# RWKV attention and GELU MLP on one core: a drain of TensorE between state and value products, replaced by a GpSimd memset that both sides wait on

## The chip, the cores and the metric

The kernel runs on one core of a Trainium2 chip. The metric is the device time of one execution in microseconds; where runs are compared, it is the median of several. The core has five engines with instruction queues of their own: TensorE (PE, matrix products; its weight loads are shown apart as PEld), VectorE (DVE), ScalarE (ACT), GpSimd (POOL) and SyncE (SP, which issues the loads and stores here). They wait for each other by semaphores only.

## What is computed

A recurrent attention over 768 tokens, for 4 batches of 8 heads of 48 channels, and an MLP with a GELU behind it, all in float32:

```python
for t in range(S):
    kt, vt, rt = (k[:, :, t], v[:, :, t], r[:, :, t])
    cur = np.einsum('bhd,bhe->bhde', u[None] * kt, vt)
    y[:, :, t] = np.einsum('bhd,bhde->bhe', rt, state + cur)
    state = w[None, :, :, None] * state + np.einsum('bhd,bhe->bhde', kt, vt)
# x: y with the heads of a token side by side, 3072 x 384
h = x @ w_in                       # 384 x 2048
g = 0.5 * h * (1.0 + erf(h / np.sqrt(2.0)))
return g @ w_out                   # 2048 x 384
```

## The kernel before

The recurrence is worked out in chunks. A **group** is one pair of heads over one chunk of 128 tokens, for all four batches; there are 6 chunks x 4 pairs = 24 groups. Within a group everything is matrix products of 48 or 64 rows on 64x64 corners of the array, in two halves of 64 tokens:

- `scores` (line 403): keys times receptances, 16 products into the PSUM banks `A` (and `own`, 16 more of the same shape, in the groups of the first two chunks). `select` then copies the entries of the past into `Am`.
- `old` (line 422): the **state products**, the state so far (`Sa`, `Sb`) times the receptances (`Tb`), 16 products of 48 rows into the bank pair `Y`.
- `new` (line 432): the **value products**, `Am` times the values (`Nb`), 16 products of 64 rows that add into the same places of `Y`. The two kinds use different rows of the array and write the same banks of `Y`; a drain stands ahead of them (line 433), which holds TensorE's queue until all products before it have ended.
- `gains` (line 415): keys times values, what the chunk adds to the state.

float32 products are two passes, so 16 products are 32 entries of the trace.

TensorE works on the MLP nearly all the time (products of 128x128 with 512 columns, lines 554 and 596: the high and low halves of activations and weights, three times each). Between them it makes a **visit** to the recurrence: `products(g, f)` (line 506) is one block of TensorE's work for two neighbouring groups, the state and value products of the earlier one, `g`, and the scores and gains of the next, `f`. The order in the block is state products of `g`, scores of `f`, drain, value products of `g`, gains of `f`. The first visit has no `g`, the last no `f`; the 19 between have both. The first four groups are worked in a prologue (`first_group`) with a block `old, new` each, without scores between.

The order on each engine is fixed when the kernel is built: `Plan` takes every block with its estimated time and what it reads and writes, plays the machine through, and writes the instructions of each queue in the order of that play. GpSimd's part in the main loop is three products of 128x384 for each group (lines 379, 381, 391), which wait for the group's load `Nb` and are needed by the visit where that group is `f` or later. The two buffers of `Nb` and `Tb` alternate: the load of the group after `f` goes into those of `g`, and waits in SP's queue until the visit has read them.

Of the kernel before, what the change touches and what calls it, by code (L numbers as in the profile page):

```python
# [9 lines left out]
F32 = mybir.dt.float32  # L10
# [17 lines left out]
HALF = 64  # L28
# [17 lines left out]
class Plan:  # L46
# [9 lines left out]
    def add(self, eng, ns, at, fn, r=(), w=()):  # L56
        n = len(self.ops)
        deps = set()
        for x in r:
            deps.add(self.writer.get(x))  # L60
            self.readers.setdefault(x, []).append(n)
        for x in w:
            deps.add(self.writer.get(x))
            deps.update(self.readers.pop(x, ()))
            self.writer[x] = n
        deps -= {None, n}
        self.ops.append((eng, ns, at, fn, deps))
        self.reads.append(set(r))
# [65 lines left out]
def rwkv_gelu_mlp(tc, rkT, rkv, wuT, uN, wmlp, r, k, vT, w, u, out):  # L134
    nc = tc.nc
    with ExitStack() as ctx:
        cst = ctx.enter_context(tc.tile_pool(name="cst", bufs=1))
# [6 lines left out]
        def sb(shape, dt, name, pool=None):  # L144
            return (pool or wk).tile(shape, dt, name=name)
# [130 lines left out]
        one = lambda x, i: x[:, :, i:i + 1]  # L276
# [73 lines left out]
        quarter = lambda x: slice(64 * x, 64 * x + D)  # L350
        heads = lambda x: slice(D * x, D * x + D)
        times = lambda h: slice(64 * h, 64 * h + 64)
# [50 lines left out]
        def scores(g, keys=None, col=0):  # L403
            for b in range(NB):
                for h in range(2):
                    for x in range(2):
                        k_ = (g.t[:, 1] if keys is None else keys)[quarter(x), b, times(h)]
                        nc.tensor.matmul(g.x[times(h), x, col + b * HALF:col + (b + 1) * HALF], lhsT=k_,  # L408
                                         rhs=g.t[quarter(x), 0, b, times(h)], start=True, stop=True)

        def own(g):
            scores(g, g.kb, U0)


        def gains(g):
            for b in range(NB):
                for x in range(2):
                    for h in range(2 if g.more else 1):
                        nc.tensor.matmul(g.u[quarter(x), h, g.u0 + b * D:g.u0 + (b + 1) * D], lhsT=g.kn[times(h), b, heads(x)],  # L419
                                         rhs=g.vn[times(h), b, heads(x)], start=True, stop=True)  # L420

        def old(g):
            for b in range(NB):
                for j in range(2):
                    for h in range(1 if g.c == 0 else 0, 2):
                        l = quarter(j ^ h)
                        nc.tensor.matmul(g.y[quarter(j), h, b * HALF:(b + 1) * HALF], lhsT=g.s[h][l, b, :],  # L427
                                         rhs=g.t[l, 0, b, times(h)], start=(b == 0 and not spreads(g)), stop=False,
                                         skip_group_check=True)


        def new(g):
            nc.tensor.drain()
            for b in range(NB):
                for j in range(2):
                    for h in range(2):
                        nc.tensor.matmul(g.y[quarter(j), h, b * HALF:(b + 1) * HALF], lhsT=g.vn[times(h), b, heads(j ^ h)],  # L437
                                         rhs=g.am[times(h), j ^ h, b, :], stop=True, skip_group_check=True,
                                         start=(g.c == 0 and h == 0 and b == 0 and not spreads(g)))


        spreads = lambda g: g.c == 0 and g.p < 3
# [63 lines left out]
        def products(g, f):  # L506


            r, w, ns = [], [], 0
            if g:  # L510
                r += [g.T, g.V, g.AM] + g.S[0] + g.S[1]
                w += g.Y
                ns += 1200
            if f:
                r += [f.T, f.K, f.V] + ([f"{f.KB}0", f"{f.KB}1"] if f.direct else [])
                w += f.X + f.U
                ns += 1300 if f.direct else 850

            def go():
                if g:  # L520
                    old(g)
                if f:
                    scores(f)
                    if f.direct:
                        own(f)
                if g:
                    new(g)
                if f:
                    gains(f)

            add("pe", ns, LATER, go, r=r, w=w)
# [57 lines left out]
        bank = lambda i: O[i] if i < 3 else YU[:, 0]  # L589
# [175 lines left out]
        with tc.If(plain[0] < 2 * LP * NP):  # L765
# [5 lines left out]
            g = general.enter_context(tc.tile_pool(name="g", bufs=2))  # L771
# [76 lines left out]
```

## Time and profile before

| | |
|---|---|
| time, median of 3 runs | 507.44 us (504.56 to 509.48) |
| span of the profiled execution | 507.7 us |
| TensorE busy with products | 486.0 us, 96% of the span |
| VectorE, ScalarE, GpSimd busy | 243.0, 205.5, 71.6 us |
| value products of the 19 visits with a next group, first start | 52.2, 73.1, 94.3, 113.7, 136.1 ... 406.5 us |
| one visit on TensorE | 2.2 us (405.25 to 407.46 in the one at 406 us) |

A row of the timeline gives a start, a length, an engine, a line of the kernel, what is written from what, and in brackets the idle time ahead of it with what ended it. Weight loads run ahead of the products that they belong to, so they overlap the products before. "Issue" stands for time in which the engine waited for nothing that the profile shows; a drain shows up as that. The ends of matrix products are modelled, their starts are measured.

### The profile page before, as it was taken

The numbers are of one execution on the slowest core, as the hardware profiler recorded it, in microseconds if no ns is written. First come the engines' busy times: TensorE is split into PE (matmuls) and PEld (weight loads), VectorE is DVE, ScalarE is ACT, GpSimd is POOL, SyncE is SP. The second block draws the span as 40 slices with busy tenths as digits, with TensorE's granted clock in tenths as the row PEclk, the third lists the DMA queues.
The fourth block names the chain that finished last, engine by engine and source line by source line (L and its number), as shares of the span: only waits on it lengthen the run. The fifth ranks groups of instructions, "written<-read, shape, count | busy, mean of one in ns | idle before, by whom it ended". The sixth has DMA issues, their size and how long they took to land.

```text
span 507.7 us, 11458 instructions
## 1 busy us (share of the span) xinstructions
PE 486.0 (96%) x5009; PEld 390.1 (77%) x5009; DVE 243.0 (48%) x366; ACT 205.5 (40%) x435; POOL 71.6 (14%) x80
## 2 busy tenths in 40 slices
PE   7879899999999999999999999999999999999995
PEld 5767677777787787777787787787787787888884
DVE  5869899998345344625254434253433231211111
ACT  3448567755442442442433443433442423322221
POOL 4220101033022022301121120220220200000000
PEclk9568999999999999999999999999999999999999
DMA  7954736622303113403023403033403000100001
GB/s 222 247 196 135 253 118 217 196 87 88 124 24 96 52 43 96 146 1 94 8 88 94 144 3 94 1 94 94 143 5 95 0 13 10 64 1 0 0 1 66
DMA packets 13190, 43.85 MB, mean 86 GB/s; under 512 B 1808, under 2 KB 2192, under 8 KB 13136
## 3 DMA queue, kind: packets, MB, share of 16 engines
q1 hardware_dynamic: 13136, 43.07, 27.3%
q8 instruction: 41, 0.67, 0.6%
q14 instruction: 13, 0.11, 0.1%
HBM read 36.38 MB, written 4.72 MB: 81 GB/s over the span
## 4 chain that ended last, share of the span: by engine, by line
PE 80%; DVE 11%; issue 3%; DMA 3%; ACT 1%; POOL 0%; SPq 0%; DVEq 0%; ACTq 0%; POOLq 0%
PE Hp L554 35%; PE O L596 34%; PE Y L437 3%; PE A L408 3%; PE Y L427 2%; DVE wa L338 2%; DVE wl L342 2%; DVE wa L336 1%; DMA raw<-in_wmlp_dram 1%; PE Y L419 1%; PE Y L596 1%; DVE Am L465 1%; DMA Nb<-in_rkv_dram 1%; DVE gl L585 1%; DVE Tb L375 1%
## 5 line engine op out<-in xcount | busy, mean ns | idle before, releaser
L554 PE MATMUL Hp<-xx,wh 128*128 128x512 f32 x576 | 168.1, 399 | 1.7 <-ACT gf L584 1.0
L585 DVE TENSOR_TENSOR gl<-gf,gh 128x512 fp32r<-128x512 f32 x95 | 71.4, 752 | 193.5 <-ACT gf L584 193.3
L583 ACT ACTIVATE gh<-Hp 128x512 fp32r<-128x512 f32 x95 | 56.9, 599 | 227.7 <-PE Hp L554 227.5
L554 PEld LDWEIGHTS Hp<-xx,wh 128*128 128x128 f32 x576 | 107.0, 189 | 27.9 <-ACT wh L340 1.8
L554 PE MATMUL Hp<-xx,wl 128*128 128x512 f32 x288 | 84.4, 400 | 1.7 <-DVE wl L342 1.7
L596 PE MATMUL O<-gh,wh 128*128 128x512 f32 (+1 forms) x285 | 82.2, 395 | 0.2 <-issue 0.2
L596 PE MATMUL O<-gh,wl 128*128 128x512 f32 (+1 forms) x285 | 80.7, 390 | 0.0
L596 PE MATMUL O<-gl,wh 128*128 128x512 f32 (+1 forms) x285 | 80.7, 390 | 0.0
L554 PEld LDWEIGHTS Hp<-xx,wl 128*128 128x128 f32 x288 | 54.0, 189 | 16.7 <-DVE wl L342 4.1
L596 PEld LDWEIGHTS O<-gh,wh 128*128 128x128 f32 x285 | 52.5, 188 | 13.0 <-issue 0.7
L596 PEld LDWEIGHTS O<-gl,wh 128*128 128x128 f32 x285 | 52.6, 188 | 11.7
L596 PEld LDWEIGHTS O<-gh,wl 128*128 128x128 f32 x285 | 52.5, 188 | 11.6
L584 ACT ACTIVATE gf<-Hp 128x512 f32<-128x512 f32 x96 | 56.9, 593 | 0.0
L379 POOL TENSOR_TENSOR Nb<-Nb 128x384 f32<-128x384 f32 x16 | 18.5, 1159 | 258.1 <-DMA Nb<-in_rkv_dram 215.8
L399 ACT ACTIVATE Am<-diag,cs 128x64 f32<-128x64 f32 x128 | 33.5, 343 | 5.1 <-DVE cs L394 5.0
L381 POOL TENSOR_TENSOR Nb<-Nb,WN 128x384 f32<-128x384 f32 x20 | 27.0, 1349 | 44.2 <-DMA Nb<-in_rkv_dram 42.9
L375 DVE TENSOR_TENSOR Tb<-Tb,E 112x1024 f32<-112x1024 f32 x20 | 25.4, 1269 | 2.0 <-DMA Tb<-in_rkT_dram 1.8
L460 DVE SCALAR_TENSOR_TENSOR Sb<-Sa,E,Y 48x192 f32<-48x192 f32 x40 | 16.5, 413 | 15.4 <-ACT xx L479 9.3
L394 DVE TENSOR_REDUCE cs<-Nb 128x8 f32<-128x384 f32 x16 | 8.8, 552 | 25.5 <-POOL Nb L391 25.5
L479 ACT CAST xx<-Y 112x512 fp32r<-112x512 f32 (+1 forms) x18 | 10.6, 587 | 25.0 <-PE Y L419 17.4
L391 POOL TENSOR_TENSOR Nb<-Nb,u_sb 128x384 f32<-128x384 f32 x16 | 17.7, 1107 | 0.1
L330 ACT ACTIVATE wa<-raw 128x768 f32<-128x768 f32 x16 | 14.6, 912 | 6.5 <-DMA raw<-in_wmlp_dram 4.7
(122 smaller groups left out, 398.8 us busy)
## 6 DMA issues: line engine op xcount, KB each, us to landing
raw<-in_wmlp_dram SPq DMA_DIRECT2D x16, 768.0 KB, 5.0
Nb<-in_rkv_dram SPq DMA_DIRECT2D x16, 576.0 KB, 5.2
Tb<-in_rkT_dram SPq DMA_DIRECT2D x20, 448.0 KB, 3.9
out_dram<-raw SPq DMA_DIRECT2D x5, 768.0 KB, 3.6
xx<-x SPq DMA_DIRECT2D x30, 64.0 KB, 2.7
T<-in_rkT_dram SPq DMA_DIRECT2D x4, 448.0 KB, 5.7
N<-in_rkv_dram SPq DMA_DIRECT2D x4, 384.0 KB, 5.1
Nb<-in_rkv_dram SPq DMA_DIRECT2D x4, 384.0 KB, 6.7
```

The lines of the kernel that those rows point to most:

```text
L375: add("dve", sdve(1024), LATER, lambda: nc.vector.tensor_tensor(out=flat, in0=flat, in1=E[:, 0, g.p].rearrange("l h i -> l (h i)").unsquee ...
L379: add("pool", pool(DM), LATER, lambda: nc.gpsimd.tensor_tensor(out=g.n[:, 0], in0=g.n[:, 0], in1=g.n[:, 1], op=ALU.mult), r=[g.K], w=[g.R])
L381: add("pool", pool(DM), LATER, lambda: nc.gpsimd.tensor_tensor(out=g.kn, in0=g.kn, in1=WN[:, g.p].rearrange("s j d -> s (j d)").unsqueeze( ...
L391: add("pool", pool(DM), LATER, lambda: nc.gpsimd.tensor_tensor(out=g.n[:, 0], in0=g.n[:, 0], in1=u_sb[:, g.p, :].unsqueeze(1).to_broadcast ...
L399: add("act", sact(HALF) + 60, LATER, lambda x=x, b=b: nc.scalar.activation(out=g.am[:, x, b, :], in_=diag2, func=AF.Copy, scale=g.sums[:, ...
L408: nc.tensor.matmul(g.x[times(h), x, col + b * HALF:col + (b + 1) * HALF], lhsT=k_, rhs=g.t[quarter(x), 0, b, times(h)], start=True, stop=True)
L460: add("dve", 420, at, lambda l=l, x=x, more=more: nc.vector.scalar_tensor_tensor(out=g.s[h + 1][quarter(1 - x)], in0=g.s[h][l], scalar=E[l ...
L554: nc.tensor.matmul(O[3], lhsT=wt[j][:, 0, k_ * 128:(k_ + 1) * 128], rhs=x[:, a, k_, :], start=start and k_ == ks[0], stop=stop and k_ == k ...
L583: add("act", 600, LATER, lambda: nc.scalar.activation(out=high, in_=O[3], func=AF.Gelu), r=["H"], w=[GH])
L584: add("act", 600, LATER, lambda: nc.scalar.activation(out=gf, in_=O[3], func=AF.Gelu), r=["H"], w=["gf"])
L585: add("dve", sdve(512), LATER, lambda: nc.vector.tensor_tensor(out=low, in0=gf, in1=high.bitcast(F32), op=ALU.subtract), r=["gf", GH], w=[GL])
L596: nc.tensor.matmul(bank(dst)[:, a:b], lhsT=wt[j][:, 1, d * 128:(d + 1) * 128], rhs=gt[:, a:b], start=(j == 0 and n == 0), stop=(j == NJ - ...
```

## The change

In a visit with both groups, `old` keeps its last product in hand; behind it, in the order of the program, GpSimd gets a memset of a tile of one element, `turn`, that waits for that product. The drain is left out, and the first value product waits for the memset instead. In the prologue's blocks and in the last visit, where no scores stand between state and value products, the drain stays.

```diff
                         l = quarter(j ^ h)
-                        nc.tensor.matmul(g.y[quarter(j), h, b * HALF:(b + 1) * HALF], lhsT=g.s[h][l, b, :],
+                        g.last = nc.tensor.matmul(g.y[quarter(j), h, b * HALF:(b + 1) * HALF], lhsT=g.s[h][l, b, :],
...
-        def new(g):
-            nc.tensor.drain()
+        turn = sb([1, 1], F32, "turn", cst)
+
+        def after(x, y):
+            tc.add_manual_dep(x.ins, y.ins.name, mybir.DependencyInfo(
+                mybir.DependencyClass.Sync, mybir.DependencyReason.DATA), reason="row tiles of one bank")
+
+        def handed(g):
+
+            g.turn = nc.gpsimd.memset(turn, 0.0)
+            after(g.turn, g.last)
+
+        def new(g, turn=None):
+            if not turn:
+                nc.tensor.drain()
             for b in range(NB):
...
-                        nc.tensor.matmul(g.y[quarter(j), h, b * HALF:(b + 1) * HALF], lhsT=g.vn[times(h), b, heads(j ^ h)],
+                        mm = nc.tensor.matmul(g.y[quarter(j), h, b * HALF:(b + 1) * HALF], lhsT=g.vn[times(h), b, heads(j ^ h)],
...
+                        if turn:
+                            after(mm, turn)
+                            turn = None
...
                 if g:
                     old(g)
+                if g and f:
+                    handed(g)
                 if f:
                     scores(f)
                     if f.direct:
                         own(f)
                 if g:
-                    new(g)
+                    new(g, f and g.turn)
```

TensorE's queue at the first visit with both groups, before, from the last state product to the first gains (in brackets the semaphores that a row waits for; drains are not among the rows, this one stands ahead of the rows of line 437):

```order
L427 MATMUL Y<-Tb_106,Sb 48x64
L408 MATMUL A<-Tb_107 64x64 [waits DMAHW7_49]
L408 MATMUL A<-Tb_107 64x64 x15
L408 MATMUL A<-Tb_107,KB_109 64x64 x16
L437 MATMUL Y<-Am_116,Nb_114 48x64 x16
L419 MATMUL Y<-Nb_115 48x48 [waits DMAHW0_49,Pool_49]
L419 MATMUL Y<-Nb_115 48x48 x15
```

The same stretch of TensorE's queue after the change, where the value products are those of line 449:

```order
L427 MATMUL Y<-Tb_106,Sb 48x64
L408 MATMUL A<-Tb_107 64x64 [waits DMAHW7_49]
L408 MATMUL A<-Tb_107 64x64 x15
L408 MATMUL A<-Tb_107,KB_109 64x64 x16
L449 MATMUL Y<-Am_116,Nb_114 48x64 [waits Pool_49]
L449 MATMUL Y<-Am_116,Nb_114 48x64 x15
L419 MATMUL Y<-Nb_115 48x48 [waits DMAHW0_49]
L419 MATMUL Y<-Nb_115 48x48 x15
```

No product moved; the wait for GpSimd stands at the first value product now, and the first product of the gains waits for its load alone.

GpSimd's queue around the first visits, as a piece of the difference (`Nb` is a group's keys and values, the products are those of lines 379 to 391):

```order
 L381 TENSOR_TENSOR Nb_115<-Nb_115,WN 128x384
+L440 MEMSET turn 1x1
 L381 TENSOR_TENSOR Nb_114<-Nb_114,WN 128x384
+L440 MEMSET turn 1x1
 L381 TENSOR_TENSOR Nb_115<-Nb_115,WN 128x384
+L440 MEMSET turn 1x1
 L379 TENSOR_TENSOR Nb_114<-Nb_114 128x384
 L381 TENSOR_TENSOR Nb_114<-Nb_114,WN 128x384
 L391 TENSOR_TENSOR Nb_114<-Nb_114,u_sb 128x384
+L440 MEMSET turn 1x1
```

Each memset stands behind the products of the group that is `f` in its visit and ahead of those of the group after it; so it goes on to the last of the 19.

## Rows read from the trace of the kernel before

**Rows 1.** The page: span, and busy time, share and instructions of each engine.

```profile
span 507.7 us, 11458 instructions
...
PE 486.0 (96%) x5009; PEld 390.1 (77%) x5009; DVE 243.0 (48%) x366; ACT 205.5 (40%) x435; POOL 71.6 (14%) x80
```

**Rows 2.** Waits of weight loads, to and from 122.5 us: total, times, longest.

```profile
PEld Hp L554 <- DVE wl L342: 4.1, 6, 1.2
...
PEld Y L427 <- issue: 5.5, 15, 0.4
PEld Y L437 <- issue: 4.0, 16, 0.3
PEld A L408 <- DVE Tb L375: 1.0, 1, 1.0
```

**Rows 3.** The drain's own line: durations in ns (min/median/max), first and last start.

```profile
L433 PEldq DRAIN  x24: 470/482/1103, 14.4 to 425.4; - x24
```

**Rows 4.** Timeline of the visit at 136 us.

```profile
135.29 0.56 PEld L408 LDWEIGHTS A<-Tb 48*64 48x64 f32 x32
...
135.31 0.22 PE L427 MATMUL Y<-Tb,Sb 48*48 48x64 f32 x1
...
136.08 0.69 DVE L585 TENSOR_TENSOR gl<-gf,gh 128x512 fp32r<-128x512 f32 x1 [3.50 <-ACT gf L584]
136.09 0.14 PEld L437 LDWEIGHTS Y<-Am,Nb 64*48 64x48 f32 x4 [0.24 <-issue]
```

**Rows 5.** Timeline of the visit at 42 us, which has no value products.

```profile
42.44 0.56 PEld L408 LDWEIGHTS A<-Tb,KB 48*64 48x64 f32 x32
...
42.91 0.47 PEld L419 LDWEIGHTS Y<-Nb 64*48 64x48 f32 x32
```

**Rows 6.** Timeline of the visit at 406 us.

```profile
405.68 0.56 PEld L408 LDWEIGHTS A<-Tb 48*64 48x64 f32 x32
...
406.51 0.52 PEld L437 LDWEIGHTS Y<-Am,Nb 64*48 64x48 f32 x32 [0.27 <-issue]
```

**Rows 7.** Timeline: ScalarE behind TensorE, ahead of the visit at 406 us.

```profile
404.45 0.86 PE L554 MATMUL Hp<-xx,wh 128*128 128x512 f32 x3
...
405.36 0.60 ACT L583 ACTIVATE gh<-Hp 128x512 fp32r<-128x512 f32 x1 [3.13 <-PE Hp L554]
```

**Rows 8.** GpSimd's small instructions: a group (last, mean ns), then a line's (min/median/max ns).

```profile
L835 POOL MEMSET const-float32-0.0<- 128x1 f32 x1 | 0.1, 99 | 0.3 <-issue 0.3
...
L215 POOL COPY N<-N x1: 713/713/713, 10.2 to 10.2; 1x1 f32<-1x1 f32 x1
...
L215 POOL COPY u_sb<-Tb x1: 178/178/178, 33.1 to 33.1; 1x1 f32<-1x1 f32 x1
```

**Rows 9.** Timeline: VectorE behind GpSimd, at 145 us.

```profile
144.34 1.01 POOL L391 TENSOR_TENSOR Nb<-Nb,u_sb 128x384 f32<-128x384 f32 x1
...
145.38 0.55 DVE L394 TENSOR_REDUCE cs<-Nb 128x8 f32<-128x384 f32 x1 [1.89 <-POOL Nb L391]
```

**Rows 10.** Timeline: TensorE behind VectorE, in the visit at 205 us.

```profile
203.19 1.55 DVE L375 TENSOR_TENSOR Tb<-Tb,E 112x1024 f32<-112x1024 f32 x1
...
204.79 0.56 PEld L408 LDWEIGHTS A<-Tb 48*64 48x64 f32 x32 [0.97 <-DVE Tb L375]
```

**Rows 11.** Waits of SP's queue (loads of a group's values).

```profile
SPq L227 <- PE Y L437: 27.4, 13, 15.3
```

**Rows 12.** Timeline of GpSimd after the visit at 136 us.

```profile
141.90 1.06 POOL L379 TENSOR_TENSOR Nb<-Nb 128x384 f32<-128x384 f32 x1 [17.49 <-DMA Nb<-in_rkv_dram]
```

**Rows 13.** The chain that ended last, 40 to 130 us: start, length, what.

```profile
94.20 0.11 issue
...
113.35 0.95 DVE wl L342
```

**Rows 14.** Timelines of VectorE: beside the long copy, and at the visit at 94 us.

```profile
9.63 1.23 DVE L375 TENSOR_TENSOR T<-T,E 112x1024 f32<-112x1024 f32 x1 [0.35 <-POOL T L215]
...
93.74 0.95 DVE L336 SCALAR_TENSOR_TENSOR wa<-raw,wa 128x768 int32<-128x768 int32 x1
```

## The prediction, before the changed kernel was run

> **What bounds the kernel now.** I read the page first. TensorE is busy for 486.0 us, 96% of the span of 507.7 us, VectorE and ScalarE for about half of it, and GpSimd for 14% [rows 1]. So the question is not which engine is the bound but where TensorE still stands still, and whether a stop taken away stays away. The waits of TensorE's weight-load queue, cut at 122.5 us, answer both. Before that point it waits for data: 4.1 us for the low halves of the weights from VectorE alone. After it there is one such wait of 1.0 us, and the rest stands under "issue": 5.5 us at the first state product of a visit and 4.0 us, 16 times, at the first value product [rows 2]. The second sum is where the change works. The drain has rows of its own: 24 of them, 482 ns in the median [rows 3].
>
> The reader should see what one drain really costs, which is not its 482 ns. In the visit at 136 us the last state product starts at 135.31; the weight loads of the 32 score products start at 135.29 (they run ahead of their products), and those of the value products at 136.09, with 0.24 us of idle ahead of them [rows 4]. The drain thus runs beside the scores for most of its time, and what stands open is the tail.
>
> What would stand there without it? The visit at 42 us has no value products, hence no drain, and goes from 32 score-like products of 48 rows straight to 32 products of 64 rows. Their weight loads start at 42.44 and 42.91, so the second group follows the first after 0.47 us; with the drain it is 136.09 - 135.29 = 0.80 us [rows 4, 5]. So **a drain costs 0.33 us of TensorE**. In four visits (205.6, 348.9, 387.3, 406.5) it is a little more: at 406 us the two weight-load groups are 406.51 - 405.68 = 0.83 us apart, 0.36 more than without [rows 6].
>
> **The change part by part.** It replaces 19 of the 24 drains, those of the visits that have both an earlier group and a next one; the four groups of the prologue and the last visit keep theirs. No other instruction moves. GpSimd gets 19 memsets of one element, each behind TensorE's last state product; the first value product waits for GpSimd. The first product of the gains drops its own wait for GpSimd, which costs nothing: it was long fulfilled, since its data are ready before the visit starts.
>
> *What the hand-off takes.* No row shows a memset behind TensorE, so I bound it by neighbours, in the visit at 136 us. The last state product ends at 135.31 + 0.22 = 135.53. ScalarE starts 0.05 us after the products that it waits for (404.45 + 0.86 = 405.31, then 405.36) [rows 7]; GpSimd would so start at 135.58. The memset lasts 0.10 us (a 128x1 memset) to 0.17 us (a 1x1 copy) [rows 8], that is to 135.68 or 135.75. VectorE starts 0.03 us after GpSimd (144.34 + 1.01 = 145.35, then 145.38), and TensorE 0.05 us after VectorE (203.19 + 1.55 = 204.74, then 204.79) [rows 9, 10]; I take 0.05: the value products may go at 135.73 to 135.80. By the row without a drain they could go at 135.29 + 0.47 = 135.76 at the earliest. The scores cover the hand-off almost exactly, from just fulfilled to 0.04 us late. I take the later end, since GpSimd's own start is the least known: 135.80 instead of 136.09, **0.29 us gained per visit**, and 0.32 in the four longer ones.
>
> *Does the gain stay?* After 122.5 us TensorE's one wait for data is that at 204.8 us, for VectorE's scaled tile [rows 2, 10]. It hangs on TensorE itself: the loads of a group wait in SP's queue until the value products of the visit before have freed their tile, 13 times and at most for 15.3 us [rows 11]; GpSimd and VectorE work on them as they land. Where the visits come earlier, this wait moves along. So the 15 visits from 136 to 406 us count in full: 11 x 0.29 + 4 x 0.32 = 4.5 us. They have cover for GpSimd too: it idles for many us around a visit (17.5 us up to its start at 141.90, for a load) [rows 12], and nothing can queue behind the memset, because the next load goes to the very tile that the value products read.
>
> *The four early visits (52, 73, 94, 114 us)* stand where weights from VectorE are the limit. The chain that ended last goes through the drain at 94.2 us (0.11 us of "issue" ahead of the value products) and in the same manner at 73.0, but at 113 us, and likewise at 52, through VectorE [rows 13]. Two count. One of them may lose: a 1x1 copy on GpSimd took 0.71 us beside a VectorE product of two SBUF tiles that ran from 9.63 to 10.86, ending as that did [rows 8, 14], and at 94 us such an instruction runs from 93.74 to 94.69, just when the memset would start (by the same steps about 93.8) [rows 14]. Held up to its end, the values would go at 94.77 instead of 94.31, a loss of 0.46; not held, a gain of 0.29. I take +0.29 for the visit at 73 us and the middle, -0.1, for this one: 0.2 us.
>
> The Trainium skill, GPSIMD Engine Reference, Specifications, says that GpSimd shares its SBUF interfaces with VectorE and that they contend when VectorE runs an instruction with two SBUF inputs; the 0.71 us copy agrees. In the later visits none runs where the memset would (VectorE idles for 3.50 us up to 136.08 [rows 4]), so by that rule the sum is the same.
>
> **Sum:** 4.5 + 0.2 = 4.7 us. The profiled execution spans 507.7 us and there is nothing to add around it; it lies 0.3 us over the median, 507.44 us. 507.44 - 4.7 = **502.7 us**, 0.93% less. A measurement of this kernel tells about 1% from no change (its three runs lie between 504.56 and 509.48).
>
> **Rivals.**
> *More than that.* If the memset is quicker than the copy, nothing is late (0.33 and 0.36), and if all four early visits count, it is 15 x 0.33 + 4 x 0.36 = 6.4 us: 501.0 us. For it: the memset's 0.10 us. Against it: the weight waits before 122.5 us, which take back what is gained there. 0.13.
>
> *Partly late.* GpSimd's answer to TensorE is shown nowhere. If the hand-off takes 0.15 us longer than I take it, the 15 visits gain 0.14 to 0.17 us each, 2.2 us in all: 505.2 us. 0.13.
>
> *Slower.* GpSimd's answer as a whole is as slow as its slow copy, in each visit: 135.58 + 0.71 + 0.05 = 136.34, 0.25 us later than now. 15 x 0.25 and the two early ones at about the same make 4.2 us more: 511.7 us. It decides from 136.09 - 135.53 = 0.56 us between the last state product and the first value product on; below it the change gains, above it loses. For it: that copy. Against: the 13 other copies of one element, at 173 to 178 ns [rows 8], and VectorE's idling at that point of the late visits [rows 4]. 0.06.
>
> *The gap is not the drain's.* The array itself may have to empty between products of 48 rows and of 64 rows; then the stop stays and the time with it, 507.4 us. Against: the visit at 42 us makes that step within 0.47 us, as closely as it goes on [rows 5]. 0.06. The Trainium skill, TensorEngine Tiling, Key Properties, says that a change of tiling mode drains TensorE; by that rule this rival holds if 48 and 64 rows are two modes, and the row at 42.9 us says that they are not.
>
> **How the numbers follow.** My forecast has 0.62, the rivals 0.13, 0.13, 0.06 and 0.06. The forecast's own range is 501.6 to 503.9 (0.07 us more or less in each visit). The range over the cases is **501.0 to 507.0**: it reaches over the partly late case and short of no gain and slower (0.12), and leaves some 0.07 at its lower end. Faster by over 1% is below 502.4 us, only 0.3 us from my number: a bit over 0.4 of the forecast's 0.62 and most of the larger gain, 0.39 in all. Slower by over 1% is the slow hand-off and a bit of scatter, 0.07. The rest, 0.54, is within 1%.
>
> **What would show it.** In the changed profile the waits at the first value product should fall from 4.0 us to under 1 us, and the two weight-load groups of the visit at 136 us should stand 0.47 to 0.51 us apart instead of 0.80. The memset should start about 0.05 us after the last state product and last 0.10 to 0.17 us. The visits after 122.5 us should come 0.29 us earlier each, so that the last, at 406.5 us, comes some 4.7 us earlier. I am wrong in the price if the groups stand further apart, with GpSimd as the releaser; wrong in the mechanism if they stand 0.8 us apart though the memset was done by 135.8; and wrong in what is kept if the visits come closer but new waits for VectorE, ScalarE or a load take the time back.

## The result, and the profile after

The changed kernel takes **499.14 us** (median of 6 runs, 497.38 to 500.26) where the kernel before, on the same chip, takes 507.81 us (6 runs, 504.56 to 509.48). That is 8.7 us less, a ratio of 0.983 with a 95% interval of 0.9804 to 0.9856. A second comparison gave 500.05 against 508.4 us, 0.9833 [0.9788, 0.9878]. The prediction was 502.7 us with a range of 501.0 to 507.0: the direction was right, but the time is 3.6 us lower than forecast and lies 1.9 us under the range.

The page of the changed kernel answers [rows 1]: the span, and each engine's busy time, share and instructions.

```profile
span 495.7 us, 11423 instructions
...
PE 478.1 (96%) x5009; PEld 386.3 (78%) x5009; DVE 241.8 (49%) x366; ACT 206.3 (42%) x435; POOL 76.8 (15%) x99
```

The products are the same 5009; GpSimd has 19 instructions more. What answers [rows 2], the waits of the weight-load queue from behind the four early visits to the end, is this (total, times, longest):

```profile
PEld Y L427 <- issue: 5.5, 15, 0.4
PEld Y L427 <- DVE Tb L375: 0.4, 1, 0.4
PEld A L673 <- issue: 0.4, 1, 0.4
PEld Y L449 <- issue: 0.3, 1, 0.3
```

The wait at the first value product fell from 4.0 us in 16 places to 0.3 us in one, the last visit, which keeps its drain. And a second row is gone: the wait of 1.0 us for VectorE's tile `Tb` (`PEld A L408 <- DVE Tb L375` of [rows 2]) has no answer here.

The new instruction's own line (durations in ns, min/median/max, first and last start), where [rows 3] had the drains:

```profile
L440 POOL MEMSET turn<- x19: 89/89/1037, 46.8 to 394.6; 1x1 f32 x19
...
  PE Y L427: 172.3, 19
...
  PEld Y L449: 0.4, 1
  PE Y L449: 0.3, 1
```

All 19 memsets wait for TensorE's state products; of the 19 first value products only one shows a wait for its memset. The fifth visit with both groups, at 136 us in [rows 4], now reads:

```profile
129.78 0.56 PEld L408 LDWEIGHTS A<-Tb 48*64 48x64 f32 x32
...
129.79 0.22 PE L427 MATMUL Y<-Tb,Sb 48*48 48x64 f32 x1
...
130.10 0.09 POOL L440 MEMSET turn<- 1x1 f32 x1 [12.17 <-PE Y L427]
130.25 0.53 PEld L449 LDWEIGHTS Y<-Am,Nb 64*48 64x48 f32 x32
130.30 0.63 PE L449 MATMUL Y<-Am,Nb 64*48 64x64 f32 x32
```

The two weight-load groups stand 130.25 - 129.78 = 0.47 us apart instead of 0.80. The memset starts 0.09 us after the last state product's modelled end (129.79 + 0.22 = 130.01), lasts 0.09 us, and is done at 130.19, 0.11 us ahead of the first value product.

Where the rest went is read from the busy times by stretch: first a stretch and its length, then the busy time (and instructions) of TensorE's products, its weight loads, VectorE, ScalarE and GpSimd, then the granted clock, the busy share of the DMA engines and their rate in GB/s. The cuts lie at the first value product of the first, fifth, eighth, ninth and last visit with both groups. The kernel before:

```profile
0.00:52.20 52.20, 42.90 (x835) 34.65 (x835) 39.38 (x67) 27.33 (x51) 11.00 (x30) 0.74 0.64 194
52.20:136.10 83.90, 79.84 (x864) 61.70 (x865) 72.71 (x101) 53.25 (x92) 11.70 (x8) 1.00 0.47 155
136.10:193.70 57.60, 57.31 (x600) 46.09 (x600) 24.54 (x41) 20.50 (x51) 10.40 (x9) 1.00 0.21 61
193.70:205.60 11.90, 10.92 (x164) 8.68 (x164) 7.18 (x10) 3.69 (x11) 3.33 (x3) 1.00 0.38 106
205.60:406.50 200.90, 199.70 (x1990) 160.28 (x1990) 79.25 (x121) 74.72 (x182) 35.12 (x30) 1.00 0.23 70
406.50:507.70 101.20, 95.29 (x556) 78.75 (x556) 19.96 (x30) 26.04 (x48) 0.00 (x0) 0.99 0.06 20
```

The changed kernel, cut at the same products:

```profile
0.00:47.50 47.50, 39.95 (x838) 32.39 (x841) 38.51 (x66) 27.33 (x51) 14.27 (x31) 0.78 0.71 214
47.50:130.30 82.80, 78.66 (x877) 61.46 (x873) 72.36 (x100) 53.54 (x92) 13.08 (x12) 1.00 0.47 157
130.30:186.90 56.60, 56.60 (x615) 45.79 (x609) 24.11 (x41) 20.62 (x52) 10.62 (x12) 1.00 0.21 62
186.90:197.40 10.50, 10.50 (x180) 8.54 (x176) 6.61 (x10) 3.93 (x12) 3.56 (x4) 1.00 0.39 115
197.40:394.80 197.40, 197.40 (x2005) 159.51 (x1998) 80.17 (x120) 74.63 (x182) 35.27 (x40) 1.00 0.23 71
394.80:495.70 100.90, 95.03 (x568) 78.58 (x558) 20.00 (x30) 26.26 (x49) 0.00 (x0) 0.99 0.06 20
```

From 130 to 395 us TensorE is now busy without a gap, by the modelled ends of its products (its busy time is the stretch's length). The third and the fifth stretch hold 3 and 10 visits and are 1.0 and 3.5 us shorter: 0.35 us a visit. The fourth holds one visit, and is 1.4 us shorter. The second, the early visits, is 1.1 us shorter, and the first 4.7 us. That last figure is not the change's: up to the first value products the two kernels differ by one drain, at the very end. Over all kernels of this study, with the drain or the memset there, the first visit starts anywhere from 47.5 to 53.1 us, at granted clocks that differ from run to run (0.74 and 0.78 here), and a second profile of the kernel before has it at 49.05 us. A median of several runs is less exposed to this scatter than one profile. From the first visit to the end it was 455.5 and 456.9 us in two profiles of the kernel before, and 448.2 and 447.2 us in two of the changed one: 8.5 us less between the means, close to the 8.7 us between the medians.

So three amounts have to be explained: about 5 us in the late visits, 1 to 2 us at the visit at 205 us, and 1 to 2 us in the early ones.

### The profile page after: what moved, and what is told of

It reads as the page before. It is cut to its first block, busy times and chain, and to the rows that moved or that the text cites. A ratio compares the mean times of both kernels' runs of the same rounds, so it can differ in the third digit from the quotient of the medians.

```text
span 495.7 us, 11423 instructions
## 1 busy us (share of the span) xinstructions
PE 478.1 (96%) x5009; PEld 386.3 (78%) x5009; DVE 241.8 (49%) x366; ACT 206.3 (42%) x435; POOL 76.8 (15%) x99
## 4 chain that ended last, share of the span: by engine, by line
PE 83%; DVE 10%; DMA 2%; issue 2%; ACT 1%; POOL 0%; SPq 0%; DVEq 0%; POOLq 0%
PE Hp L571 36%; PE O L613 35%; PE Y L427 3%; PE Y L449 3%; DVE wa L338 2%; PE A L408 2%; DVE wl L342 2%; DVE wa L336 1%; DVE gl L602 1%; DMA raw<-in_wmlp_dram 1%; PE Y L419 1%; PE Y L613 1%; DMA N<-in_rkv_dram 1%; PE Y L462 1%; DVE Sb L475 1%
## 5 line engine op out<-in xcount | busy, mean ns | idle before, releaser
L379 POOL TENSOR_TENSOR Nb<-Nb 128x384 f32<-128x384 f32 x16 | 17.5, 1095 | 108.1 <-DMA Nb<-in_rkv_dram 82.5
L381 POOL TENSOR_TENSOR Nb<-Nb,WN 128x384 f32<-128x384 f32 x20 | 28.9, 1443 | 16.6 <-DMA Nb<-in_rkv_dram 15.4
L440 POOL MEMSET turn<- 1x1 f32 x19 | 3.1, 161 | 172.3 <-PE Y L427 172.3
L375 DVE TENSOR_TENSOR Tb<-Tb,E 112x1024 f32<-112x1024 f32 x20 | 25.7, 1284 | 4.1 <-DMA Tb<-in_rkT_dram 4.0
```

What stands on the lines that cost most here:

```text
L375: add("dve", sdve(1024), LATER, lambda: nc.vector.tensor_tensor(out=flat, in0=flat, in1=E[:, 0, g.p].rearrange("l h i -> l (h i)").unsquee ...
L379: add("pool", pool(DM), LATER, lambda: nc.gpsimd.tensor_tensor(out=g.n[:, 0], in0=g.n[:, 0], in1=g.n[:, 1], op=ALU.mult), r=[g.K], w=[g.R])
L381: add("pool", pool(DM), LATER, lambda: nc.gpsimd.tensor_tensor(out=g.kn, in0=g.kn, in1=WN[:, g.p].rearrange("s j d -> s (j d)").unsqueeze( ...
```

## Experiments

The kernels are the two of the comparison with a line or two changed. Each comparison has its own runs of the kernel before, which vary in their median from 507.1 to 508.4 us; ratios are against those.

**Drain and memset together.** The changed kernel with the drain put back, so that the memset and the moved waits are there, and the drain as well.

```diff
         def new(g, turn=None):
-            if not turn:
-                nc.tensor.drain()
+            nc.tensor.drain()
```

> The changed kernel with the drain put back in the 19 visits: the memset, its wait and the value product's wait on it stay, so queues and semaphores are those of the changed kernel. If the gain of 8.7 us is the drain's (theory A), it is gone: within 1 us of the kernel before, and the weight loads of scores and values stand 0.80 us apart again. If a part of it comes from the waits that moved (GpSimd's products lost their wait for TensorE, the gains lost theirs for GpSimd; theory B), about 3.5 us stay.

Measured: 505.30 us (12 runs), ratio 0.9971 [0.9947, 0.9994]. Its timeline of the fifth visit, and its waits of the weight-load queue in the late part:

```profile
133.78 0.56 PEld L408 LDWEIGHTS A<-Tb 48*64 48x64 f32 x32
...
134.11 0.09 POOL L440 MEMSET turn<- 1x1 f32 x1 [12.17 <-PE Y L427]
134.58 0.52 PEld L448 LDWEIGHTS Y<-Am,Nb 64*48 64x48 f32 x32 [0.24 <-issue]
```

```profile
PEld Y L448 <- issue: 4.0, 16, 0.3
```

The 0.80 us and the 4.0 us are back, though the memset was done 0.38 us ahead of the value products. The stop is the drain's and not the array's. The length of a late visit, from the start of its first state product to that of its last gains product, tells the drain apart from the rest of the edit: in the median 2.06 us before and with both, 1.73 us in the changed kernel. The drain is worth 0.33 us a visit: 0.29 us between the last score and the first value product (329 ns instead of 38 from start to start), the rest in the first value products behind the stop. The moved waits are worth nothing that shows: a separate wait instruction of TensorE ahead of the gains, 51 ns long, is there 24 times before and 5 times with the memset, and the visits with both are as long as those before.

The ten intervals from 205 to 406 us add up to 200.9 us before, 200.6 with both and 197.4 after (197.3 in the second profile), so 0.03 us of the 0.35 an interval lies outside the visits. It is in the MLP products between them, which take up to 0.5% longer in the kernel before (16.75 us against 16.67 between the visits at 253 and 272 us). It is not the separate wait: the kernel with early visits alone, below, keeps that wait in all its late visits and has 200.6 us too, and the long memset, which lacks it, has 16.74 us between those two visits. Why these products are slower in some kernels is open.

In all, the kernel takes 1.5 us less [0.3, 2.7] with every drain in place, by the median more than these 0.3 us. What else it lost is the wait at the visit at 205 us.

**Late visits alone, early visits alone, and the kernel before again.**

```diff
-                if g and f:
+                if g and f and f.gi >= 9:
                     handed(g)
...
-                    new(g, f and g.turn)
+                    new(g, f and f.gi >= 9 and g.turn)
```

This is the late half (the visits from 136 us on); the early half has `f.gi < 9`, and the third kernel is the one before, unchanged.

> Memset instead of drain in the 15 visits from 136 us on, drain in the four early ones. The trace of the changed kernel shows 0.34 us less in each of these visits, so theory A, with the late visits counting in full and nothing else, gives 5.1 us less than before; if the stall of 1.0 us in the visit at 205 us goes too, 6.1 us. If the early visits carry the rest (theory C), this stays at 5 to 6 us and the early-only kernel has the missing 3 us; if the rest is the scatter of the prologue (theory D), this one comes out at 5 to 8 us with prologues of different length in the two traces.

> Memset instead of drain in the four visits up to 114 us, drain in the 15 later ones. Prediction: two of the four count and one may lose, 0.2 us. Theory C (the early visits give back more than their drains, since VectorE's weight work moves with them) says 2 to 4 us; theory A with D says 0 to 1 us.

> The kernel before, word for word, as a second trace and a null. Its ratio should be 1.00 within 0.3%. Open is what its trace shows at two places where the first one differed from the changed kernel's outside the visits: the first visit's value products at 52.2 us against 47.4 us, and the wait of 1.0 us in the visit at 205 us. If both recur (theory B or C), they belong to the kernel; if the prologue's length and the wait differ from the first trace (theory D), they are scatter.

Measured: late visits alone 500.78 us, 0.9894 [0.9845, 0.9944]; early visits alone 505.87 us, 0.9957 [0.9927, 0.9987]; before again 507.19 us, 1.0008 [0.9979, 1.0037]. The late visits carry 5.4 us [2.8, 7.9], the early ones 2.2 us [0.7, 3.7]; both figures hold the wait at 205 us, which both kernels had lost. The kernel before again had it (1.31 us from the last state product to the first score). So that wait vanished with any of these edits, also with those that leave the drains around it, or all drains, in place.

What do they share? Each has fewer instructions on TensorE (10,100 recorded before, 10,062 after, 10,081, 10,070 and 10,092 in the three above). That pointed at the instructions themselves. The table of DMA queues has a queue of its own for them (packets, MB, share of 16 engines; the kernel before):

```profile
q1 hardware_dynamic: 13136, 43.07, 27.3%
q8 instruction: 41, 0.67, 0.6%
```

41 packets of 16 KB for some 10,100 instructions of TensorE; one takes 0.9 to 2.0 us in the trace. The Trainium skill, Runtime: NRT & Kernel Launch, Instruction fetch mechanics, says that an engine's sequencer fetches its instructions by its own DMA queue in blocks of 16 KiB, at a cost that is mostly hidden; size and count agree. No row here shows TensorE waiting for one. But in the kernel before one of them begins 2.9 us after the issue of the load of `Nb` at 194.51 us. A load lands in 16 parts: 15 of this one land within 4.29 us, the last after 5.61. Behind it stands a chain: GpSimd takes up the group 0.13 us after the last part, at 200.25 us, VectorE follows, and TensorE waits for VectorE's `Tb` until 204.79 us [rows 10].

**Moving the packet.** Two kernels to test that: drains behind the warm-up products, 60 in the kernel before and 50 in the changed one, shift the program against the 16 KB blocks. Nothing else differs.

```diff
             for n in range(HEATS):
                 heat((A + [YU[:, 0], YU[:, 1]] + [AE[:, 0], AE[:, 1]])[n % 6])
+            for n in range(60):
+                nc.tensor.drain()
```

> The kernel before, with 60 drains of TensorE behind the warm-up products; nothing else differs. Traces so far: in the two executions of the kernel before, a packet of 16 KB that brings TensorE's instructions falls at 197.4 and 193.2 us, 2.9 and 1.7 us after the issue of a group's load, whose 16 parts then land over 2.65 and 4.06 us, and TensorE waits in the visit behind it (1.04 and 1.31 us from the last state product to the first score, where 0.04 is usual). In the four kernels with memsets the packet falls clear of that load, its parts land within 1.3 us, and the wait is gone. 60 instructions more ahead of it bring the packet some 60 instructions earlier in the program, which is in or before the visit, 0.3 to 0.7 us ahead of the load's issue. Theory (the packet delays the load): the parts land within 1.3 us and the wait falls under 0.1 us; the interval from the visit ahead to this one falls from 11.9 to 12.8 us to about 10.8 us. Rival (the drain itself, or the visits' timing, makes the wait): the wait stays at 1.0 us or more, with the packet elsewhere. The time: 1.0 to 2.0 us less by the theory, unchanged by the rival, and in both up to 2 us more for the 60 drains if nothing in the prologue covers them; 504 to 508 us.

> The changed kernel, with 50 drains of TensorE behind the warm-up products. In the changed kernel the instruction packet falls at 195.9 us, 8.3 us behind the issue of the load at 187.6 us; 50 instructions more ahead of it should bring it to about 3 us behind the issue, into the load, as in the kernel before. Theory (the packet delays the load): the load's parts land over 2 us or more, and TensorE waits 0.5 to 1.3 us in the visit behind it, though no drain stands in it. Rival (it hung on the drain): no wait, wherever the packet falls. The time: 499.1 plus 0.5 to 1.5 us by the theory, 499.1 by the rival, and in both up to 2 us more for the drains in the prologue.

Measured: 508.37 us, 1.0003 [0.9975, 1.0031], and 502.94 us (the median of five runs from 499.2 to 503.8 us, by which the ratio goes; a sixth took 508.5), 0.989 [0.9842, 0.9938]. In the changed kernel the packet came into the load, 0.84 us behind the issue where about 3 us was expected, and the wait came back, though no drain stands in these visits. The three intervals between the visits ahead of it are those of the changed kernel within 0.01 us (18.87, 18.86 and 18.87 us), so TensorE kept its pace there. The timeline, and the wait as a row of the late part's waits:

```profile
194.21 1.25 POOL L381 TENSOR_TENSOR Nb<-Nb 128x384 f32<-128x384 f32 x1 [6.97 <-DMA Nb<-in_rkv_dram]
...
196.58 0.55 DVE L396 TENSOR_REDUCE cs<-Nb 128x8 f32<-128x384 f32 x1 [2.00 <-POOL Nb L393]
...
197.05 1.55 DVE L377 TENSOR_TENSOR Tb<-Tb,E 112x1024 f32<-112x1024 f32 x1
...
198.65 0.56 PEld L410 LDWEIGHTS A<-Tb 48*64 48x64 f32 x32 [1.28 <-DVE Tb L377]
```

```profile
PEld A L410 <- DVE Tb L377: 1.3, 1, 1.3
```

GpSimd stood waiting for the load, whose 16th part landed 5.99 us after its issue, at 194.07 us; VectorE waited for GpSimd, and TensorE for VectorE. In the changed kernel the last part is there 3.98 us after the issue, and `Tb` is ready 0.47 us before TensorE asks for it.

In the kernel before the packet did not get out of the load: it moved from 2.9 and 1.6 us to 0.7 us behind the issue, the wait stayed (0.81 us), and so did the time. My expectation for it was wrong on where 60 instructions would bring the packet, so that kernel does not test what it was made for. A packet does not move in proportion to the instructions: early visits alone, with 8 fewer than before, has it at 7.6 us, the first visit alone (below), with 2 fewer, at 3.1. The changed kernel with the drains took 2.9 us more than the changed kernel again, measured beside it (502.94 against 500.05 us). The wait is 1.3 us of that, and up to 2 us were expected for the drains themselves; the split is not shown.

All twelve profiles of this place, from the trace's landing records (us after the load's issue; "late" is the 16th part behind the 15th; the wait is from the last state product to the first score, 0.04 at least):

| kernel | drains at this visit | packet at | late | wait | from the visit before |
|---|---|---|---|---|---|
| before | yes | 2.9 | 1.3 | 1.04 | 11.88 |
| before, again | yes | 1.6 | 2.1 | 1.31 | 12.79 |
| before, 60 drains ahead | yes | 0.7 | 1.1 | 0.81 | 11.67 |
| after, 50 drains ahead | no | 0.8 | 1.8 | 1.35 | 11.83 |
| drain and memset | yes | -0.9 and 7.3 | 0.3 | 0.04 | 10.81 |
| early alone | yes | -0.5 and 7.6 | 0.5 | 0.04 | 10.80 |
| first visit alone (below) | yes | 3.1 | 0.4 | 0.04 | 10.82 |
| late alone | no | -0.5 and 7.5 | 0.4 | 0.04 | 10.46 |
| all but the first (below) | no | -0.5 and 7.3 | 0.1 | 0.04 | 10.46 |
| after | no | -0.5 and 8.3 | 0.2 | 0.04 | 10.46 |
| after, again | no | -0.5 and 7.6 | 0.1 | 0.04 | 10.46 |
| long memset (below) | no | -1.1 and 7.1 | 0.2 | 0.04 | 10.89 |

The wait goes with the packet and not with the drain: three kernels with drains there have no wait, and one without drains has it. Where a packet starts 0.7 to 2.9 us behind the issue, one part of sixteen is 1.1 to 2.1 us late; at 3.1 us, or outside, it is not. The kernel with 50 drains is the only one in which a move made for the purpose brought the packet in or out; in the others it moved along with the edit. The three loads issued next are late by one part as well where this one is (0.8 to 1.0 us before, 1.9 us before again, 0.6 us with the 60 drains, 0.8 us with the 50). That fits a single DMA engine that serves the packet first; the trace does not name the engine of a packet, so this last step is inferred. The Trainium skill, DMA: Bandwidth & Descriptors, Queues, rings and completion order, says that a DMA engine turns from one queue to another only after a whole packet; the trace agrees in size: the packets in the four late loads took 0.95, 2.03, 1.33 and 1.58 us (in the order of the table), and the part was 1.3, 2.1, 1.1 and 1.8 us late.

**The first visit.** The early visits gained more than the 0.3 us a visit that their drains cost. From the first to the second visit it is 20.9, 21.0, 20.9 and 21.4 us in four profiles with plain drains in the first visit, and 19.3 to 20.4 us in five with memsets. The same signature stands in it: a load of MLP weights is issued as the first visit's value products start, and with the drain its 16th part lands 0.9 to 2.6 us after the others. ScalarE waits for this load. Two kernels, with `f.gi == 5` (the memset in the first visit alone) and `f.gi != 5` (everywhere but there) in the two conditions shown above:

> The kernel before, with the memset in place of the drain in the first visit (the value products at about 50 us) alone; the other 18 visits keep their drains. From the profiles so far: from the value products of the first visit to those of the second it is 20.9 to 21.4 us where the first visit has a drain and 19.3 to 20.4 us where it has the memset; in the kernels with a drain there, TensorE's instruction packet falls 1.1 to 1.6 us behind the issue of a weight load, one of whose 16 parts lands 1.4 to 1.8 us after the other 15, and ScalarE waits for that load. With the memset the value products come 0.3 us earlier, the packet falls 0.5 us behind the issue, and the 16th part lands with the others. Theory (the drain of the first visit shifts the packet into the load): the 16th part within 0.3 us of the 15th, the interval 19.3 to 20.2 us, the time 1.0 to 1.6 us under the kernel before, of which the visit itself is 0.3; the later visits keep 329 ns of gap. Rival (the early difference is scatter, or comes from the second to fourth visit's own drains): the interval 20.9 us or more, the time within 0.3 us of before.

> The changed kernel with the drain back in the first visit (at about 48 us) alone; 18 visits have the memset. Theory (the drain of the first visit shifts the instruction packet into the weight load): the packet 1.1 to 1.6 us behind the load's issue, its 16th part over 1 us late, the interval from the first to the second visit 20.5 us or more where it was 19.3 to 20.1, and the time 1.0 to 1.6 us above the changed kernel, 500.3 to 501.5 us. Rival (the early difference comes from the second to fourth visit, or is scatter): the interval stays at 19.3 to 20.1 us, the time within 0.4 us of the changed kernel.

Measured: first visit alone 504.29 us, 0.9948 [0.992, 0.9976]; all but the first 500.58 us, 0.9871 [0.9821, 0.9921]. Taking out one drain of 19 gives 2.6 us [1.2, 4.1], where 1.0 to 1.6 was expected. ScalarE's waits between the first two visits, and TensorE's behind them (total, times, longest), with the drain in the first visit alone:

```profile
ACT wa L330 <- DMA raw<-in_wmlp_dram: 3.1, 1, 3.1
PEld Hp L571 <- ACT gf L601: 1.5, 1, 1.5
```

and in the changed kernel, again, where the second of the two rows does not occur:

```profile
ACT wa L330 <- DMA raw<-in_wmlp_dram: 1.9, 2, 1.4
```

| kernel | first visit | packet behind the load's issue | 16th part late | to the second visit | the same without the second visit's gap |
|---|---|---|---|---|---|
| before / again | drain | 1.6 / 1.1 | 1.8 / 1.6 | 20.91 / 20.98 | 20.58 / 20.65 |
| all but the first | drain | 1.3 | 1.7 | 20.66 | 20.62 |
| late alone | drain | 1.1 | 1.4 | 20.86 | 20.53 |
| drain and memset | both | 0.9 | 0.9 | 20.64 | 20.11 |
| early alone | memset | 0.8 | 1.1 | 20.36 | 20.32 |
| first visit alone | memset | 0.8 | 0.5 | 20.31 | 19.98 |
| after / again | memset | 0.5 / 0.5 | 0.1 / 0.2 | 20.08 / 19.29 | 19.55 / 18.95 |
| after, 50 drains ahead | memset | 0.2 | 0.2 | 19.28 | 18.94 |
| long memset | memset | 0.5 | 0.2 | 19.58 | 19.54 |
| before, 60 drains ahead | drain | 0.1 | 2.6 | 21.42 | 21.09 |

The interval holds what the second visit itself loses between its last score and its first value product (0.04 us with a memset that comes in time, 0.33 with a drain, 0.34 and 0.53 with a held memset); the last column leaves that out. It rises with the lateness: 18.9 to 19.6 us at 0.1 or 0.2 us, 20.0 to 20.3 at 0.5 to 1.1, 20.5 to 20.7 at 1.4 to 1.8, 21.1 at 2.6. Between profiles of the same lateness 0.6 us stay open.

Without the drain the value products come earlier against the load, which is issued 0.41 us behind the first of them instead of 0.10. The packet goes with the products, so it comes nearer to the issue, and in the profiles that have it 0.5 us behind, the part is no longer late. The direction held in both kernels, the size less so: 0.6 us less of interval with the memset in the first visit alone, where the packet came only to 0.8 us, and 0.6 to 1.4 us more with the drain there alone (1.1 to 1.7 by the last column). The rest of the 2.6 us of the first visit alone is the drain's own 0.3 us and the wait at 205 us, which is gone in that kernel too (the table above). The last line speaks against the simple story: there the packet comes 0.1 us behind the issue and one part is the latest of all. So it is shown that the first interval goes with the late part. That the packet makes the part late is not shown here, nor that a packet right behind the issue is harmless; what made the part late in that one kernel is open.

**A longer memset**, to see how much room the scores leave and what GpSimd's answer costs.

```diff
-        turn = sb([1, 1], F32, "turn", cst)
+        turn = sb([1, 512], F32, "turn", cst)
```

> The changed kernel with a memset of 512 elements of one partition instead of one element; the order on all engines is the same. In the changed kernel the memset is done 104 ns ahead of the first value product. If a memset of 512 elements takes L us instead of 0.09, the value products should come L - 0.19 us later plus what GpSimd's answer takes on the way to TensorE (0.05 us by the answer of VectorE to TensorE): with L = 0.53, about 0.39 us later in each of the 19 visits, so 15 x 0.39 = 5.9 us more in the late ones and 505 to 507 us in all. By the theory that the hand-off is hidden, GpSimd must now show as the releaser of the first value product in every visit, and the distance from the memset's end to that product is the answer's own price, 0.05 us or less. Rival (the scores leave far more room than 0.1 us, so that the price of the hand-off is nothing): under 1 us more, 499 to 500 us.

> The changed kernel once more, unchanged, for a second profiled execution and a narrower ratio. By the sum over visits of the first profile (15 late visits at 0.33 us, 5.1 us; the wait at 205 us gone, 1.1 to 2.0 us; early visits between -0.2 and +0.3 us each) it should be 6 to 8 us below the kernel before, 499 to 501 us. Theory (early visits gain little, the rest of the first comparison was scatter of the prologue): nearer to 501. Rival (early visits carry a few us): 498.5 to 499.5.

Measured: 506.33 us, 0.9971 [0.9941, 1.0002]; the changed kernel again 500.05 us. A late visit of the long memset:

```profile
132.50 0.51 POOL L440 MEMSET turn<- 1x512 f32 x1 [11.20 <-PE Y L427]
133.07 0.52 PEld L449 LDWEIGHTS Y<-Am,Nb 64*48 64x48 f32 x32 [0.33 <-POOL turn L440]
```

GpSimd is now the releaser, with 514 ns of memset, and the value products follow 54 ns after its end (in the rows 133.07 - 132.50 - 0.51 = 0.06). The memset's own line counts those who wait for it:

```profile
L440 POOL MEMSET turn<- x19: 514/514/582, 49.7 to 403.0; 1x512 f32 x19
...
  PEld Y L449: 5.0, 15
```

It is 15 times, the late visits; the early ones cover the longer memset, three by their second set of scores and the fourth by a wait of 0.49 us ahead of its scores. That is the answer's price, which the trace of before could not show: 0.09 us to start, 0.05 us back. With the one-element memset's 0.09 us the hand-off takes 0.23 us behind the last state product's end, and the scores hold TensorE for 0.29 us: it fits with 0.05 us to spare. With the long one the value products came 0.375 us later in each late visit, and the visit took 0.41 us longer (2.14 against 1.73 us): 15 x 0.41 = 6.2 us, of the 6.3 us between the medians. The second run of the changed kernel fits neither of the two theories set for it better than the other; 1 to 2 us for the early visits is what the profiles show.

## Why the prediction was right, and where it was wrong

The direction and the mechanism of the late visits were right, the time lies under the range. Three steps of the sum failed: the wait at 205 us was put at nothing and gave 1.1 to 2.0 us, the early visits were put at 0.2 us and gave 1.1 to 2.1, and the price of a late visit was put at 0.29 us and is 0.33.

- **The mechanism held.** The stop was the drain's; without it the weight-load groups stand 0.47 us apart, as at 42 us [rows 5]. The three rivals that end above the forecast are out: nothing is partly late, the answer is not slow, and the array does not empty by itself.
- **The price per visit was too low.** I took the later end for the hand-off, 0.04 us late, hence 0.29 us. It is not late: GpSimd starts 0.04 us later than taken from ScalarE [rows 7], but its memset lasts 0.09 us and not 0.17, as the copy of [rows 8]. The rival price of 0.33 us was right, that of 0.36 in four visits nearly: most late visits are 2.058 - 1.732 = 0.326 us shorter, those three that differ 0.345. The dropped wait ahead of the gains cost nothing, as forecast. 15 visits x 0.33 = 4.9 us instead of 4.5, and 0.3 us came from the MLP products between the visits, for which the sum had no term.
- **The wait at 205 us** is the step that failed on its kind: "Where the visits come earlier, this wait moves along". It was no wait of the chain through TensorE. It came from one late part of a load. Beside it ran a packet of TensorE's instructions, and the change, which drops 38 instructions, moved the packets. It gave 1.1 to 2.0 us (11.88 and 12.79 to 10.46, less 0.34 for the visit; in the second profile 0.65 of it is at an MLP product that waits for `xx`, another late load). What should have made me look were [rows 2] and [rows 10] together: one such wait among 15 visits that are otherwise alike.
- **The early visits** were put at 0.2 us; the stretch from the first to the fifth visit is 1 to 2 us shorter (83.9 and 84.1 us before, 82.8 and 82.0 after). Of that, 0.8 to 1.7 us lie in the first interval, which goes with the late weight load, and 0.3 us in the three behind it, of the 1.0 us that the three drains in them cost. The loss that I looked for at 94 us did not occur. The memset there is held, 0.42 us, but beside a `TENSOR_SCALAR` (87.85 to 88.40 us) and not the `SCALAR_TENSOR_TENSOR` that I had named, and the visit's second set of 16 score products (`own`) covers it. The named instruction did not hold the memset where the two met: in the kernel with the long one it ran right through, in 0.52 us against 0.51 elsewhere:

```profile
90.50 1.81 DVE L336 SCALAR_TENSOR_TENSOR wa<-raw,wa 128x768 int32<-128x768 int32 x2
90.63 0.52 POOL L440 MEMSET turn<- 1x512 f32 x1 [11.29 <-PE Y L427]
```

  One visit earlier, at 73 us before, the holding is longer than that cover. Its timeline after the change:

```profile
66.09 0.56 PEld L408 LDWEIGHTS A<-Tb 48*64 48x64 f32 x32
...
66.46 1.02 DVE L334 TENSOR_SCALAR wa<-wa 128x768 int32<-128x768 int32 x2
66.47 1.04 POOL L440 MEMSET turn<- 1x1 f32 x1 [9.34 <-PE Y L427]
66.55 0.56 PEld L408 LDWEIGHTS A<-Tb,KB 48*64 48x64 f32 x32
...
67.56 0.52 PEld L449 LDWEIGHTS Y<-Am,Nb 64*48 64x48 f32 x32 [0.45 <-POOL turn L440]
```

  A memset of one element lasts 1.04 us beside two VectorE instructions of one SBUF input each, and ends with them; the value products wait 0.45 us, 0.2 us more than for the drain (530 ns from the last score to the first value product, 329 with a drain). The prediction weighed such a holding, but in another visit and beside an instruction that shows none.
- **The base.** The run lasts 1.7 us more than its span (497.38 against 495.7), where I had put nothing around it. By the same 1.7 us the profiled execution of before, 507.7 us, is the slowest of its runs (509.48), 2 us over the median. The sum, a difference, did not suffer.

In all: forecast 4.7 us; found, from the first visit on and between the means of two profiles each, 8.5 us: 1.6 up to the fifth visit, 4.9 in the 14 late intervals (4.6 in the visits, 0.3 in the MLP products), 1.5 for the wait at 205 us, and 0.5 behind the last visit, which is within the scatter of that stretch over all kernels (100.8 to 101.5 us with drains in the late visits, 100.9 to 101.3 with memsets). The rival "more than that", 6.4 us, had the right price for the late visits and still lacked the two loads.

## What to carry to other kernels

When one wait stands alone among many like places, ask for its cause before you call it structural: look whether one part of a load landed late, and what else moved through the DMA engines then. A drain costs what of it the work ahead does not cover, here 0.33 us of 0.48. A hand-off through an idle engine (0.23 us) is hidden where it fits under that work; look first whether a neighbour can hold that engine. And an edit of a few instructions on a long queue can move the packets that bring all that follow, as it did here, so a difference of 1 to 2 us in a kernel like this one needs a second kernel with the same code placed otherwise before it is put down to the edit.

## What was not expected of the hardware

- A packet of 16 KB with TensorE's instructions (41 in a run, 0.9 to 2.0 us each) goes with one part in 16 of a load landing 0.5 to 2.1 us behind the others when it begins about 0.7 to 2.9 us after the load's issue. One profile, with the packet at 0.1 us and the part 2.6 us late, does not fit. Two such loads go with 1.1 to 2.0 us of the kernel before at 205 us and 1.0 to 1.7 us ahead of the second visit.
- A memset of one element on GpSimd takes 88 to 90 ns. Beside a `TENSOR_SCALAR` of VectorE with one SBUF input it took 0.16 to 0.17, 0.85 to 1.04 and 0.42 to 0.45 us in the first three visits and ended 0.03 us after that instruction, or after the second of two; in two profiles (early alone, all but the first) it began within 0.05 us of that instruction's start and took 88 ns. The Trainium skill, GPSIMD Engine Reference, Specifications, names, besides two SBUF inputs, VectorE instructions in a 2-port performance mode as what GpSimd contends with; that would fit, but no row shows an instruction's mode. Beside the `SCALAR_TENSOR_TENSOR` with two SBUF inputs shown above, the memset was not slower.
- GpSimd starts 0.09 us after the modelled end of the product that it waits for, and TensorE 0.05 us after GpSimd; 512 elements on one partition take 0.51 us.
